# Decode attention on one core: other pieces of the K and V stream, and the last head finished on VectorE and SyncE

## The chip, the cores and the metric

The kernel runs on one core of a Trainium2 chip. The metric is the device time of one execution in microseconds (us). The core has a TensorE (PE, with its weight loads shown as PEld), a VectorE (DVE), a ScalarE (ACT), a GpSimd (POOL) and a SyncE (SP). SP and ACT each issue transfers on a queue of their own; 16 DMA engines carry them.

## The reference

```python
B, H, Sq, Sk, D = 1, 16, 1, 8192, 256      # q, k, v in bf16
scale = q.shape[-1] ** -0.5
scores = jnp.einsum("bhqd,bhkd->bhqk", q, k) * scale
p = _softmax(scores, axis=-1)
return jnp.einsum("bhqk,bhkd->bhqd", p, v)
```

There is one query per head. K and V of a head are 8192 x 256 in bf16, 4 MB each, so 16 heads read 128 MB. Every byte is used once.

## The kernel before

**Layout.** A head's 8192 keys lie as 128 partitions x 64 columns (J = 64); a column is 256 values, 512 bytes, in each partition. There are two buffers for K and two for V, chosen by the parity of the head, each 4 MB.

**The stream.** SP issues all loads in the order of the list `stream`. An entry is (k or v, head, first column, end column, semaphore). From head 2 on, the first piece of a load waits until its buffer is free: for K until VectorE is done with head h - 2 (`kd`), for V until TensorE has finished the output of head h - 2 (`pv`). SP stands at such a wait, with all later loads behind it. k0 comes in three pieces (`K_FIRST`), v0, v1 and v13 in halves, v14 in four pieces and v15 in nine (`V_LATE`), each later piece with a semaphore of its own (`V_SEMS`). From head 2 on the list goes k(h+2), v(h).

**Scores.** VectorE multiplies 48 columns of K with q and sums each (L191, one instruction per column). The last 16 columns go over TensorE: it transposes them (`ktrans`, L280), ScalarE copies them out of PSUM (L376), TensorE multiplies with q (`kscore`, L294), and ScalarE adds these scores to VectorE's (`scopy`, L380). VectorE's last column waits for that.

**Softmax.** VectorE takes the maximum per partition (`m`, L207), TensorE transposes it (`transpose_m`, L228), VectorE takes the maximum of that (`xmax`, L173), TensorE spreads it (`bcast`, L234), ScalarE takes the exponential and its sum (`expo`, L384 and L388), TensorE adds the sums (`total`, L244), and VectorE takes the reciprocal (`recips`, L178). In VectorE's program an even head runs the maximum of the head before at its column 40; an odd head has the reciprocal and the maximum of the head before at columns 2 and 3.

**Output.** `pv` (L259) multiplies 64 columns of V with the exponentials, one matmul per column, into a PSUM row of 256. `final` on ScalarE multiplies that with the reciprocal into `o_sb` (L401) and issues the store of 512 bytes (L408). TensorE works in a loop of nine turns: scores of an even head, output of the even head before, scores of the odd head, output of the odd head before. In the even output the softmax steps of the odd head before lie after columns 32, 48 and 64.

**Waits for pieces of V.** The loop's code is the same in each turn, and so are the waits in it. Before, a wait for a later piece compares a semaphore, which starts at 16, with a register: 16 in the early turns, 32 in the turn that needs the piece:

```python
fin_turn = pe.snap((i // 8) * 16 + 16)
half_turn = pe.snap(((i + 1) // 8) * 16 + 16)
```

**The end.** After its loop ScalarE finishes heads 14 and 15 with `final`, waits for both stores and stops.

Of the kernel before, what the change touches and what calls it, by code (L numbers as in the profile page):

```python
# [10 lines left out]

NPE = 16
GRP = 4
K_FIRST = (16, 32)
V_HALVED = 13
V_LATE = {14: (0, 16, 32, 48), 15: (0, 16, 28, 38, 46, 52, 57, 60, 62)}
AHEAD = {"kd": 1, "sc": 1, "sp": 2, "ex": 2, "m": 1, "g": 1, "mT": 1, "l": 2, "bc": 1, "nb": 1, "rc": 2, "pv": 2, "fin": 4}
V_SEMS = (("va0", "v0b", "v0c", "v0d"), ("va1", "v1b", "v1c", "v1d", "v1e", "v1f", "v1g", "v1i", "v1j"))


class _Step:
# [19 lines left out]
def bass_standalone__mha_softmax__decode_kernel(nc: bass.Bass, q: bass.AP, k: bass.AP, v: bass.AP, out: bass.AP):  # L41
# [3 lines left out]
    J = Sk // P  # L45
# [3 lines left out]
    NG = NPE // GRP  # L49
    JD = J - NPE  # L50
    QW = D + NH
    HALF = J // 2
    dt = k.dtype

    stream = [("k", 0, 0, K_FIRST[0], "k0"), ("k", 0, K_FIRST[0], K_FIRST[1], "k0a")]
    stream += [("k", 0, K_FIRST[1], J, "k0b"), ("k", 1, 0, J, "k1")]
    stream += [("v", 0, 0, HALF, "va0"), ("k", 2, 0, J, "k0"), ("v", 0, HALF, J, "v0c")]
    stream += [("v", 1, 0, HALF, "va1"), ("k", 3, 0, J, "k1"), ("v", 1, HALF, J, "v1c")]  # L60
    for h in range(2, H):
        if h + 2 < H:
            stream.append(("k", h + 2, 0, J, f"k{h % 2}"))
        if h in V_LATE:
            for (a, b), name in zip(zip(V_LATE[h], V_LATE[h][1:] + (J,)), V_SEMS[h % 2]):
                stream.append(("v", h, a, b, name))
        elif h == V_HALVED:
            stream += [("v", h, 0, HALF, "va1"), ("v", h, HALF, J, "v1h")]
        else:
            stream.append(("v", h, 0, J, f"va{h % 2}"))  # L70

    with contextlib.ExitStack() as ctx:
# [28 lines left out]
        identb = sb("identb", [P, P], BF16)  # L101
        ones_row = sb("ones_row", [1, P], FP32)
        ones_col = sb("ones_col", [P, 1], FP32)
        o_sb = [sb(f"o_sb{i}", [1, D], out.dtype) for i in range(2)]

        acc = [ps(f"acc{i}", [P, 512]) for i in range(2)]
# [3 lines left out]
        sm = ps("sm", [P, 512])  # L110
        qps = ps("qps", [P, 512])

        for name in ("qc", "pool", "cb", "cf", "qp", "qs", "qb", "kd", "tp", "kt", "sp", "sc", "m", "mT", "g", "bc", "nb", "ex"):
            sem(name)
        for name in ("l", "rc", "pv", "fin", "ldq", "k0", "k0a", "k0b", "k1", "va0", "va1", "v1h", "o0", "o1"):
            sem(name)
        late = [name for row in V_SEMS for name in row[1:] if name not in ("v0c", "v1c")] + ["v1h"]
        for row in V_SEMS:
            for name in row[1:]:
                sem(name)  # L120

        def src(t, h):
            return t[0, h].rearrange("(p j) d -> p (j d)", p=P)

        if True:

            @(lambda f: f(nc.sync))
            def _(sp):
                for kind, h, a, b, name in stream:
                    buf = (kbuf if kind == "k" else vbuf)[h % 2]  # L130
                    if h >= 2 and a == 0:
                        if kind == "k":
                            sp.wait_ge(sem("kd"), h)
                        else:
                            sp.wait_ge(sem("pv"), h + 1)
                    sp.dma_start(  # L136
                        buf[:, a * D : b * D], src(k if kind == "k" else v, h)[:, a * D : b * D]
                    ).then_inc(sem(name), 16)
                sp.nop()

            @(lambda f: f(nc.gpsimd))
            def _(pool):
                def step(ins, n):
                    ins.then_inc(sem("pool"), 1)
                    pool.wait_ge(sem("pool"), n)

                def eye(t, n, done):
                    step(pool.memset(t[:, :], 0.0), n)
                    pool.affine_select(
                        out=t[:, :],  # L150
                        in_=t[:, :],
                        compare_op=ALU.not_equal,
                        fill=1.0,
                        base=0,
                        pattern=[[-1, P]],
                        channel_multiplier=1,
                    ).then_inc(sem(done), 1)

                eye(identb, 1, "cb")
                eye(ident, 2, "cf")  # L160
                pool.memset(ones_row[:, :], 1.0).then_inc(sem("cf"), 1)
                pool.memset(ones_col[:, :], 1.0).then_inc(sem("cf"), 1)
                pool.memset(q_all[:, H * QW : (H + 1) * QW], 0.0).then_inc(sem("cf"), 1)
                for name, n in AHEAD.items():
                    pool.nop().then_inc(sem(name), n)
                for name in late + ["o0", "o1", "va0", "va1"]:
                    pool.nop().then_inc(sem(name), 32 if name in ("o0", "o1") else 16)

            @(lambda f: f(nc.vector))
            def _(dve):  # L170
# [9 lines left out]
                def head(h, at):  # L180
                    dve.wait_ge(sem("qb"), h.of(1, 1))
                    dve.wait_ge(sem("ex"), h.of(1, 1))
                    dve.wait_ge(sem(f"k{h.par}"), h.of(8, 16 - 8 * h.par))  # L183
                    buf = kbuf[h.par]
                    for j in range(JD):
                        if j in K_FIRST and h.par == 0:
                            dve.wait_ge(sem("k0a" if j == K_FIRST[0] else "k0b"), 16)
                        if j == JD - 1:

                            dve.wait_ge(sem("sc"), h.of(1, 2))  # L190
                        ins = dve.tensor_tensor_reduce(  # L191
                            out=buf[:, j * D : (j + 1) * D],
                            in0=buf[:, j * D : (j + 1) * D],
                            in1=q_now[h.par][:, 0:D],
                            scale=SCALE,
                            scalar=0.0,
                            op0=ALU.mult,
                            op1=ALU.add,
                            accum_out=S[h.par][:, j : j + 1],
                        )  # L200
                        if j in at:
                            at[j]()
                    ins.then_inc(sem("kd"), 1)
                    if JD in at:
                        at[JD]()
                    dve.wait_ge(sem("kd"), h.of(1, 2))
                    dve.tensor_reduce(m[:, h.par : h.par + 1], S[h.par][:, :], AX.X, ALU.max).then_inc(sem("m"), 1)  # L207
# [12 lines left out]
                recips(last.back(1))  # L220
                xmax(last)
                recips(last)

            @(lambda f: f(nc.tensor))
            def _(pe):
# [23 lines left out]
                        stop=True,  # L249
                    ).then_inc(sem("l"), 1)  # L250

                def pv(h, waits, at):

                    pe.wait_ge(sem("fin"), h.of(1, 3))
                    pe.wait_ge(sem(f"va{h.par}"), h.of(8, 32 - 8 * h.par))
                    for j in range(J):
                        for name, value in waits.get(j, ()):
                            pe.wait_ge(sem(name), value)
                        ins = pe.matmul(  # L259
                            acc[h.par][0:1, 0:D],  # L260
                            lhsT=E[h.par][:, j : j + 1],
                            rhs=vbuf[h.par][:, j * D : (j + 1) * D],
                            start=(j == 0),
                            stop=(j == J - 1),
                        )
                        if j == J - 1:
                            ins.then_inc(sem("pv"), 1)
                        if j + 1 in at:
                            at[j + 1]()
# [75 lines left out]
                pe.wait_ge(sem("cf"), 4)  # L345
                with pe.Fori(0, H // 2 + 1) as i:
                    ev, od = _Step(0, i), _Step(1, i)
                    fin_turn = pe.snap((i // 8) * 16 + 16)
                    half_turn = pe.snap(((i + 1) // 8) * 16 + 16)
                    old = od.back(2)  # L350
                    with pe.If(i < H // 2):
                        scores(ev)
                    with pe.If(i > 0):
                        pv(
                            ev.back(2),
                            {V_LATE[14][n]: [(V_SEMS[0][n], fin_turn)] for n in range(1, len(V_SEMS[0]))},
                            {32: lambda: transpose_m(old), 48: lambda: bcast(old), 64: lambda: total(old)},
                        )
                    with pe.If(i < H // 2):
                        scores(od, before=ev)  # L360
                    with pe.If(i > 0):
                        waits = {V_LATE[15][n]: [(V_SEMS[1][n], fin_turn)] for n in range(1, len(V_SEMS[1]))}
                        waits[HALF] = [("v1h", half_turn)]
                        pv(old, waits, {})
                    with pe.If(i < H // 2):
                        total(ev)

# [1 line left out]
            def _(act):  # L369
# [83 lines left out]
                                    )  # L453
                                    final(t.back(3 - d), flat[:, bass.ds(at, D)])
                expo(_Step(H - 1))
                for h in (H - 2, H - 1):
                    final(_Step(h), out[0, h, 0:1, :])
                for i in range(2):
                    act.wait_ge(sem(f"o{i}"), 16 * (H // 2 + 2))
                act.nop()  # L460


# [26 lines left out]
```

## Time and profile before

| | us |
|---|---|
| median of 3 runs | 320.18 (320.08 to 320.52) |
| the profiled execution | 320.12 |
| its span, first to last instruction | 318.6 |
| VectorE busy | 275.2 |
| TensorE matmuls busy | 219.2 |
| ScalarE busy | 92.5 |
| bytes moved | 134.29 MB, mean 422 GB/s |

The span begins with the first instruction in the profile and ends with the last. The profiled execution is 1.5 us longer than its span. A row of the timeline gives start, duration, engine, line, operation, out<-in, count, and in brackets the idle time before it and what ended it. A row of groups gives the busy time, the mean of one in ns, and the idle time before.

### The profile page before, as it was taken

How to read it: one execution, taken by the hardware profiler on the slowest of the kernel's cores; microseconds unless marked ns; L12 is line 12 of the kernel's file. 1: busy time of each engine (PE TensorE's matmuls, PEld its weight loads, DVE VectorE, ACT ScalarE, POOL GpSimd, SP SyncE). 2: the span in 40 equal slices, each digit the busy share in tenths (PEclk: the TensorE clock that was granted, in tenths of full speed). 3: DMA queues.
4: the chain of work that ended last, by engine and by line, in shares of the span. 5: the costliest groups of instructions: out<-in, count | busy, mean ns of one | idle time of the engine just before them, and what ended most of it. 6: DMA issues, size and time to landing. Idle time of an engine off the chain costs nothing.

```text
span 318.6 us, 6833 instructions
## 1 busy us (share of the span) xinstructions
PE 219.2 (69%) x2163; PEld 156.0 (49%) x2163; DVE 275.2 (86%) x1584; ACT 92.5 (29%) x172; POOL 1.6 (0%) x11
## 2 busy tenths in 40 slices
PE   4446185988775947949387482975739668497987
PEld 1335163656553634727256262663626446266664
DVE  3989999999999898897988979799798897979920
ACT  5436050333215050330505114051330603306010
POOL 1000000000000000000000000000000000000000
PEclk9999999659797875957879597695977859699999
DMA  7999999999999999999999999999999999999995
GB/s 303 447 418 465 393 455 407 448 416 448 412 448 428 428 444 411 453 412 453 420 436 440 416 448 407 453 416 449 424 432 444 411 449 416 444 405 428 419 416 201
DMA packets 6981, 134.29 MB, mean 422 GB/s; under 512 B 800, under 2 KB 1216, under 8 KB 1856
## 3 DMA queue, kind: packets, MB, share of 16 engines
q1 hardware_dynamic: 6912, 134.22, 98.6%
q8 instruction: 2, 0.03, 0.0%
q10 hardware_dynamic: 64, 0.02, 0.0%
q14 instruction: 3, 0.02, 0.0%
HBM read 134.23 MB, written 0.01 MB: 421 GB/s over the span
## 4 chain that ended last, share of the span: by engine, by line
DMA 64%; PE 19%; DVE 15%; SPq 1%; issue 1%; ACT 0%; DVEq 0%; ACTq 0%
DMA vbuf<-in_v_dram 58%; PE acc L259 18%; DVE kbuf L191 14%; DMA kbuf<-in_k_dram 7%; SPq L136 1%; DVE S L191 0%; DVE g L173 0%; PE sm L234 0%; ACT o_sb L401 0%; DVE recip L178 0%; DVEq L209 0%; DVEq L183 0%; PE qps L244 0%; DVE m L207 0%; ACTq L400 0%
## 5 line engine op out<-in xcount | busy, mean ns | idle before, releaser
L191 DVE CUSTOM_DVE_ANT_0 kbuf<-kbuf,q_now 128x256 bf16<-128x256 bf16 x768 | 268.4, 409 | 21.3 <-DMA kbuf<-in_k_dram 20.4
L259 PE MATMUL acc<-vbuf,E 128*1 128x256 bf16 x1024 | 147.1, 313 | 41.6 <-DMA vbuf<-in_v_dram 41.4
L259 PEld LDWEIGHTS acc<-vbuf,E 128*1 128x1 bf16 x1024 | 95.5, 95 | 86.2 <-DMA vbuf<-in_v_dram 44.4
L376 ACT ACTIVATE KT<-tp 128x1024 bf16<-128x1024 bf16 x64 | 62.3, 1021 | 46.4 <-PE tp L280 45.9
L191 DVE DVE_READ_ACCUMULATOR2_ANT S<- 128x1 f32 x768 | 55.2, 72 | 0.0
L280 PE MATMUL tp<-identb,kbuf 128*128 128x128 bf16 x512 | 42.2, 239 | 14.7 <-DMA kbuf<-in_k_dram 14.5
L280 PEld LDWEIGHTS tp<-identb,kbuf 128*128 128x128 bf16 x512 | 33.6, 107 | 18.1 <-DMA kbuf<-in_k_dram 12.1
L294 PE MATMUL spe<-q_now,KT 128*128 128x1 bf16 x512 | 22.9, 166 | 27.3 <-ACT KT L376 27.0
L294 PEld LDWEIGHTS spe<-q_now,KT 128*128 128x128 bf16 x512 | 18.1, 99 | 35.7 <-ACT KT L376 26.1
L401 ACT ACTIVATE o_sb<-acc,recip 1x256 bf16<-1x256 f32 x16 | 7.3, 458 | 87.0 <-PE acc L259 85.7
L384 ACT ACTIVATE negb<-sm 128x1 f32<-128x1 f32 x16 | 2.8, 174 | 83.8 <-PE sm L234 83.8
L173 DVE TENSOR_REDUCE g<-mx 1x1 f32<-1x128 f32 x16 | 4.4, 276 | 7.5 <-PE mx L228 7.5
L234 PE MATMUL sm<-g,ones_row 1*128 1x1 f32 x32 | 6.5, 268 | 5.0 <-DVE g L173 5.0
L228 PE MATMUL mx<-ident,m 128*1 128x128 f32 x32 | 6.5, 287 | 4.3 <-DVE m L207 4.3
L234 PEld LDWEIGHTS sm<-g,ones_row 1*128 1x128 f32 x32 | 5.1, 198 | 7.1 <-DVE g L173 5.6
L371 ACT ACTIVATE q_now<-q_all 128x258 bf16 x16 | 6.7, 418 | 0.1
L178 DVE RECIPROCAL recip<-qps 1x1 f32<-1x1 f32 x16 | 2.4, 152 | 3.9 <-PE qps L244 3.9
L388 ACT ACTIVATE E<-S,negb 128x64 bf16<-128x64 f32 x16 | 5.6, 348 | 0.5
L336 PE MATMUL acc<-q_sb,identb 16*128 16x256 bf16 x16 | 4.3, 404 | 0.8 <-ACT q_all L426 0.8
L228 PEld LDWEIGHTS mx<-ident,m 128*1 128x1 f32 x32 | 2.1, 82 | 5.1 <-DVE m L207 4.8
L426 ACT ACTIVATE q_all<-acc 128x512 bf16<-128x512 f32 x8 | 4.3, 592 | 0.6 <-PE acc L336 0.6
L380 ACT ACTIVATE S<-spe 128x16 f32<-128x16 f32 x16 | 2.9, 184 | 3.6 <-PE spe L294 3.6
(24 smaller groups left out, 18.5 us busy)
## 6 DMA issues: line engine op xcount, KB each, us to landing
kbuf<-in_k_dram SPq DMA_DIRECT2D x15, 4096.0 KB, 20.3
vbuf<-in_v_dram SPq DMA_DIRECT2D x11, 4096.0 KB, 28.7
vbuf<-in_v_dram SPq DMA_DIRECT2D x6, 2048.0 KB, 24.4
vbuf<-in_v_dram SPq DMA_DIRECT2D x5, 1024.0 KB, 14.8
kbuf<-in_k_dram SPq DMA_DIRECT2D x2, 1024.0 KB, 5.8
kbuf<-in_k_dram SPq DMA_DIRECT2D x1, 2048.0 KB, 11.3
vbuf<-in_v_dram SPq DMA_DIRECT2D x1, 768.0 KB, 10.2
vbuf<-in_v_dram SPq DMA_DIRECT2D x1, 640.0 KB, 11.3
```

The lines of the kernel that those rows point to most:

```text
L173: dve.tensor_reduce(g[0:1, h.par : h.par + 1], mx[0:1, 0:P], AX.X, ALU.max).then_inc(sem("g"), 1)
L191: ins = dve.tensor_tensor_reduce(out=buf[:, j * D : (j + 1) * D], in0=buf[:, j * D : (j + 1) * D], in1=q_now[h.par][:, 0:D], scale=SCALE, ...
L228: pe.matmul(mx[0:1, 0:P], lhsT=m[:, h.par : h.par + 1], rhs=ident[:, :], start=True, stop=True).then_inc(sem("mT"), 1)
L234: pe.matmul(sm[:, 0:1], lhsT=ones_row[0:1, 0:P], rhs=g[0:1, h.par : h.par + 1], start=True, stop=True,).then_inc(sem("bc"), 1)
L259: ins = pe.matmul(acc[h.par][0:1, 0:D], lhsT=E[h.par][:, j : j + 1], rhs=vbuf[h.par][:, j * D : (j + 1) * D], start=(j == 0), stop=(j == J ...
L280: ins = pe.transpose(tp[gi % 2][:, b * D + hf * P : b * D + (hf + 1) * P], buf[:, j * D + hf * P : j * D + (hf + 1) * P], identb[:, :],)
L294: ins = pe.matmul(spe[:, c : c + 1], lhsT=KT[gi % 2][:, b * D + hf * P : b * D + (hf + 1) * P], rhs=q_now[h.par][:, D + hf : D + hf + 1], ...
L336: ins = pe.matmul(acc[pair % 2][:, (h % 2) * D : (h % 2 + 1) * D], lhsT=identb[0:H, h : h + 1].to_broadcast([H, P]), rhs=q_sb[:, :], start ...
L371: act.activation(out=q_now[h.par][:, :], in_=src_q, func=ACT.Copy).then_inc(sem("qb"), 1)
L376: act.activation(out=KT[gi % 2][:, :], in_=tp[gi % 2][:, :], func=ACT.Copy).then_inc(sem("kt"), 1)
L388: act.activation(out=E[h.par][:, :], in_=S[h.par][:, :], func=ACT.Exp, bias=negb[:, h.par : h.par + 1], scale=1.0, accum_out=lsum[:, h.par ...
L401: act.activation(out=o_sb[h.par][0:1, :], in_=acc[h.par][0:1, 0:D], func=ACT.Copy, scale=recip[0:1, h.par : h.par + 1],).then_inc(sem("fin ...
```

## The change

The stream is cut in other pieces. k0 comes as columns 0 to 16 and 16 to 64. v0 and v1 are whole, and the first loads go k0, k1, v0, k2, v1, k3. v13 is cut at 34, v14 at 24 and 44, v15 at 20, 34, 44, 52, 58 and 62. The waits of `pv` for later pieces compare with the constant 16; GpSimd gives each of these semaphores a count in advance for the heads that have no such piece, and the matmul behind each wait takes 16 away. The last head's output is multiplied by the reciprocal on VectorE into a tile of its own, `o_last`, and SP issues its store, behind all loads, and waits for it.

```diff
-K_FIRST = (16, 32)
-V_HALVED = 13
-V_LATE = {14: (0, 16, 32, 48), 15: (0, 16, 28, 38, 46, 52, 57, 60, 62)}
+K_FIRST = 16
+V_LATE = {13: (0, 34), 14: (0, 24, 44), 15: (0, 20, 34, 44, 52, 58, 62)}
+V_SEMS = {13: ("va1", "v1c"), 14: ("va0", "v0b", "v0c"), 15: ("va1", "v1b", "v1c", "v1d", "v1e", "v1f", "v1g")}
-V_SEMS = (("va0", "v0b", "v0c", "v0d"), ("va1", "v1b", "v1c", "v1d", "v1e", "v1f", "v1g", "v1i", "v1j"))
...
-    stream = [("k", 0, 0, K_FIRST[0], "k0"), ("k", 0, K_FIRST[0], K_FIRST[1], "k0a")]
-    stream += [("k", 0, K_FIRST[1], J, "k0b"), ("k", 1, 0, J, "k1")]
-    stream += [("v", 0, 0, HALF, "va0"), ("k", 2, 0, J, "k0"), ("v", 0, HALF, J, "v0c")]
-    stream += [("v", 1, 0, HALF, "va1"), ("k", 3, 0, J, "k1"), ("v", 1, HALF, J, "v1c")]
+    stream = [("k", 0, 0, K_FIRST, "k0"), ("k", 0, K_FIRST, J, "k0b"), ("k", 1, 0, J, "k1")]
+    stream += [("v", 0, 0, J, "va0"), ("k", 2, 0, J, "k0"), ("v", 1, 0, J, "va1"), ("k", 3, 0, J, "k1")]
...
-        elif h == V_HALVED:
-            stream += [("v", h, 0, HALF, "va1"), ("v", h, HALF, J, "v1h")]
...
+        o_last = sb("o_last", [1, D], out.dtype)
...
+        late = {}
+        for h, names in V_SEMS.items():
+            for name in names[1:]:
                 sem(name)
+                late[name] = late.get(name, 16 * H // 2) - 16
...
+                sp.wait_ge(sem("end"), 1)
+                sp.dma_start(out[0, H - 1, 0:1, :], o_last[0:1, :]).then_inc(sem("end"), 16)
+                sp.wait_ge(sem("end"), 17)
                 sp.nop()
...
-                for name in late + ["o0", "o1", "va0", "va1"]:
-                    pool.nop().then_inc(sem(name), 32 if name in ("o0", "o1") else 16)
+                for name, n in list(late.items()) + [("o0", 32), ("o1", 32), ("va0", 16), ("va1", 16)]:
+                    pool.nop().then_inc(sem(name), n)
...
-                        if j in K_FIRST and h.par == 0:
-                            dve.wait_ge(sem("k0a" if j == K_FIRST[0] else "k0b"), 16)
+                        if j == K_FIRST and h.par == 0:
+                            dve.wait_ge(sem("k0b"), 16)
...
                 recips(last)
+                dve.wait_ge(sem("rc"), H + AHEAD["rc"])
+                dve.wait_ge(sem("pv"), H + AHEAD["pv"])
+                dve.tensor_scalar(
+                    out=o_last[0:1, :],
+                    in0=acc[last.par][0:1, 0:D],
+                    scalar1=recip[0:1, last.par : last.par + 1],
+                    scalar2=None,
+                    op0=ALU.mult,
+                ).then_inc(sem("end"), 1)
...
-                def pv(h, waits, at):
+                def pv(h, at):
 
+                    parts = dict(zip(V_LATE[H - 2 + h.par][1:], V_SEMS[H - 2 + h.par][1:]))
...
-                        for name, value in waits.get(j, ()):
-                            pe.wait_ge(sem(name), value)
+                        if j in parts:
+                            pe.wait_ge(sem(parts[j]), 16)
...
+                        if j in parts:
+                            ins.then_inc(sem(parts[j]), -16)
...
-                for h in (H - 2, H - 1):
-                    final(_Step(h), out[0, h, 0:1, :])
-                for i in range(2):
-                    act.wait_ge(sem(f"o{i}"), 16 * (H // 2 + 2))
+                final(_Step(H - 2), out[0, H - 2, 0:1, :])
+                act.wait_ge(sem("o0"), 16 * (H // 2 + 2))
+                act.wait_ge(sem("o1"), 16 * (H // 2 + 1))
```

More of the change, by code (lines that the diff above doesn't have):

```diff
@@ L51, in bass_standalone__mha_softmax__decode_kernel @@
     QW = D + NH
-    HALF = J // 2
     dt = k.dtype
-    stream = [("k", 0, 0, K_FIRST[0], "k0"), ("k", 0, K_FIRST[0], K_FIRST[1], "k0a")]
-    stream += [("k", 0, K_FIRST[1], J, "k0b"), ("k", 1, 0, J, "k1")]
-    stream += [("v", 0, 0, HALF, "va0"), ("k", 2, 0, J, "k0"), ("v", 0, HALF, J, "v0c")]
-    stream += [("v", 1, 0, HALF, "va1"), ("k", 3, 0, J, "k1"), ("v", 1, HALF, J, "v1c")]
+    stream = [("k", 0, 0, K_FIRST, "k0"), ("k", 0, K_FIRST, J, "k0b"), ("k", 1, 0, J, "k1")]
+    stream += [("v", 0, 0, J, "va0"), ("k", 2, 0, J, "k0"), ("v", 1, 0, J, "va1"), ("k", 3, 0, J, "k1")]
     for h in range(2, H):
@@ L64, in bass_standalone__mha_softmax__decode_kernel @@
         if h in V_LATE:
-            for (a, b), name in zip(zip(V_LATE[h], V_LATE[h][1:] + (J,)), V_SEMS[h % 2]):
+            for (a, b), name in zip(zip(V_LATE[h], V_LATE[h][1:] + (J,)), V_SEMS[h]):
                 stream.append(("v", h, a, b, name))
-        elif h == V_HALVED:
-            stream += [("v", h, 0, HALF, "va1"), ("v", h, HALF, J, "v1h")]
         else:
@@ L111, in bass_standalone__mha_softmax__decode_kernel @@
         qps = ps("qps", [P, 512])
-        for name in ("qc", "pool", "cb", "cf", "qp", "qs", "qb", "kd", "tp", "kt", "sp", "sc", "m", "mT", "g", "bc", "nb", "ex"):
+        for name in ("qc", "pool", "cb", "cf", "qp", "qs", "qb", "kd", "end", "tp", "kt", "sp", "sc", "m", "mT", "g", "bc", "nb", "ex"):
             sem(name)
-        for name in ("l", "rc", "pv", "fin", "ldq", "k0", "k0a", "k0b", "k1", "va0", "va1", "v1h", "o0", "o1"):
+        for name in ("l", "rc", "pv", "fin", "ldq", "k0", "k0b", "k1", "va0", "va1", "o0", "o1"):
             sem(name)
-        late = [name for row in V_SEMS for name in row[1:] if name not in ("v0c", "v1c")] + ["v1h"]
-        for row in V_SEMS:
-            for name in row[1:]:
+        late = {}
+        for h, names in V_SEMS.items():
+            for name in names[1:]:
                 sem(name)
+                late[name] = late.get(name, 16 * H // 2) - 16
         def src(t, h):
@@ L347, in _ @@
                     ev, od = _Step(0, i), _Step(1, i)
-                    fin_turn = pe.snap((i // 8) * 16 + 16)
-                    half_turn = pe.snap(((i + 1) // 8) * 16 + 16)
                     old = od.back(2)
@@ L355, in _ @@
                             ev.back(2),
-                            {V_LATE[14][n]: [(V_SEMS[0][n], fin_turn)] for n in range(1, len(V_SEMS[0]))},
                             {32: lambda: transpose_m(old), 48: lambda: bcast(old), 64: lambda: total(old)},
@@ L361, in _ @@
                     with pe.If(i > 0):
-                        waits = {V_LATE[15][n]: [(V_SEMS[1][n], fin_turn)] for n in range(1, len(V_SEMS[1]))}
-                        waits[HALF] = [("v1h", half_turn)]
-                        pv(old, waits, {})
+                        pv(old, {})
                     with pe.If(i < H // 2):
```

## The prediction

> **What bounds the kernel now.** I read the page first: which engine is full, which chain ended last.
>
> ```profile
> span 318.6 us, 6833 instructions
> ...
> PE 219.2 (69%) x2163; PEld 156.0 (49%) x2163; DVE 275.2 (86%) x1584; ACT 92.5 (29%) x172; POOL 1.6 (0%) x11
> ...
> PEclk9999999659797875957879597695977859699999
> DMA  7999999999999999999999999999999999999995
> ...
> q8 instruction: 2, 0.03, 0.0%
> q14 instruction: 3, 0.02, 0.0%
> ...
> DMA vbuf<-in_v_dram 58%; PE acc L259 18%; DVE kbuf L191 14%; DMA kbuf<-in_k_dram 7%; SPq L136 1%; DVE S L191 0%; DVE g L173 0%; PE sm L234 0%; ACT o_sb L401 0%; DVE recip L178 0%; DVEq L209 0%; DVEq L183 0%; PE qps L244 0%; DVE m L207 0%; ACTq L400 0%
> ...
> L191 DVE CUSTOM_DVE_ANT_0 kbuf<-kbuf,q_now 128x256 bf16<-128x256 bf16 x768 | 268.4, 409 | 21.3 <-DMA kbuf<-in_k_dram 20.4
> ```
>
> The transfers are busy in every slice but the first and the last; VectorE (DVE) comes second. So the time is a start, one unbroken stream of 128 MB, and a tail, and a change counts only if it alters the number of pieces in the stream, opens a hole in it, or alters the tail. The timeline gives the pace of the stream wherever a consumer waited for a landing:
>
> ```profile
> 13.03 1.86 PE L280 MATMUL tp<-identb,kbuf 128*128 128x128 bf16 x16 [3.96 <-DMA kbuf<-in_k_dram]
> 23.25 1.63 PEld L280 LDWEIGHTS tp<-identb,kbuf 128*128 128x128 bf16 x16 [0.62 <-DMA kbuf<-in_k_dram]
> 38.79 1.89 PE L280 MATMUL tp<-identb,kbuf 128*128 128x128 bf16 x16 [8.53 <-DMA kbuf<-in_k_dram]
> ...
> 121.47 6.05 PE L259 MATMUL acc<-vbuf,E 128*1 128x256 bf16 x32 [4.62 <-DMA vbuf<-in_v_dram]
> 140.90 10.06 PE L259 MATMUL acc<-vbuf,E 128*1 128x256 bf16 x64 [3.71 <-DMA vbuf<-in_v_dram]
> ...
> 286.63 1.07 PE L280 MATMUL tp<-identb,kbuf 128*128 128x128 bf16 x16 [0.20 <-DMA kbuf<-in_k_dram]
> 296.42 3.65 PE L259 MATMUL acc<-vbuf,E 128*1 128x256 bf16 x32 [0.77 <-DMA vbuf<-in_v_dram]
> 308.85 8.04 PE L259 MATMUL acc<-vbuf,E 128*1 128x256 bf16 x64 [0.55 <-DMA vbuf<-in_v_dram]
> ```
>
> Between 121.47 and 140.90 land two whole heads (k7, v5): 9.715 us per 4 MB. The two halves of v13 take 296.42-286.63 = 9.79, 0.08 more for one extra piece. From 296.42 to 308.85 five 1 MB pieces land (v14 and the first of v15): 2.486 each, 9.94 for a head in four pieces, 0.23 more for three extra pieces. So a further piece costs 0.077 us of stream.
>
> The tail, with PE's weight loads showing the landing of each piece of v15:
>
> ```profile
> 310.74 1.18 PEld L259 LDWEIGHTS acc<-vbuf,E 128*1 128x1 bf16 x12 [0.28 <-DMA vbuf<-in_v_dram]
> 312.32 0.96 PEld L259 LDWEIGHTS acc<-vbuf,E 128*1 128x1 bf16 x10 [0.41 <-DMA vbuf<-in_v_dram]
> 313.62 0.74 PEld L259 LDWEIGHTS acc<-vbuf,E 128*1 128x1 bf16 x8 [0.34 <-DMA vbuf<-in_v_dram]
> 314.63 0.52 PEld L259 LDWEIGHTS acc<-vbuf,E 128*1 128x1 bf16 x6 [0.27 <-DMA vbuf<-in_v_dram]
> 315.41 1.18 PEld L259 LDWEIGHTS acc<-vbuf,E 128*1 128x1 bf16 x12 [0.26 <-DMA vbuf<-in_v_dram]
> 316.97 0.47 ACT L401 ACTIVATE o_sb<-acc,recip 1x256 bf16<-1x256 f32 x1 [8.15 <-PE acc L259]
> 317.47 0.24 ACTq L408 DMA_DIRECT2D out_dram<-o_sb  x1
> ```
>
> PE keeps pace until 315.41; then the last 12 columns run without a wait. Estimate: the last 7 columns of the stream take 7/64 x 9.715 = 1.06 us after 315.41, so the stream ends at about 316.45. PE is done some 0.45 later (ScalarE starts at 316.97), and 1.63 us go from there to the span's end. The last landing to the end is about 2.1 us. The transfers of this window, in 40 slices of 0.215 us, show one thing more:
>
> ```profile
> DMA  9999999999999999999953322120000000000000
> ```
>
> From 314.5 on only 0.2 to 0.3 of the 16 engines work: four engines end about 1.5 us after the others, and the last decides.
>
> **The change, part by part.**
>
> *Pieces.* The stream goes from 48 transfers to 42: k0, v0, v1 and v14 lose one each, v15 two; v13 keeps two. Four at 0.077 are -0.31 us. In v15, the five pieces from 308.85 to 315.41 carry 41 columns in 6.56 us against 41/64 x 9.715 = 6.22, 0.07 per piece; but two of the small last pieces go, where the estimate above needed no extra at all. So between 0 and -0.14 for two; I take -0.07. Together -0.38.
>
> *Start.* VectorE has 16 columns of k0 as before, at 0.35 us each (268.4/768):
>
> ```profile
> 5.54 0.42 DVE L191 CUSTOM_DVE_ANT_0 kbuf<-kbuf,q_now 128x256 bf16<-128x256 bf16 x1 [5.54 <-DMA kbuf<-in_k_dram]
> 22.26 0.33 SPq L136 DMA_DIRECT2D kbuf<-in_k_dram  x1
> 40.27 0.33 SPq L136 DMA_DIRECT2D kbuf<-in_k_dram  x1
> 57.96 0.33 SPq L136 DMA_DIRECT2D kbuf<-in_k_dram  x1
> 59.69 0.33 SPq L136 DMA_DIRECT2D vbuf<-in_v_dram  x1
> 75.69 0.33 SPq L136 DMA_DIRECT2D kbuf<-in_k_dram  x1
> ```
>
> They end at 11.1. The rest of k0 is now one piece and is there at 12.95 (PE sees it at 13.03 now), so VectorE stands 1.85 us and k2 is issued at 24.1, not 22.26. This is hidden: v0, now whole and ahead of k2, keeps the queue full until about 33.6 (23.25 + 10.35, with the lateness that k2 shows at 38.79). k3 is issued 16.9 after head 1 starts, at about 41.4; v1 fills the queue until 53.
>
> *Order.* The first places are now k1, v0, k2, v1, k3, k4. k2 lands about 43.5 (38.79 + half a head), k3 at 62.9. Head 2 starts at 43.6, and 17.0 to 17.1 us after the landing of its k its buffer is free: the issue of k4 comes at 60.6. Here, without v1's second half between k3 and k4, the queue holds 2.3 us of work. What must be covered is issue to flow: 0.74 to 5.54 was 4.8 us for k0's first 1 MB at 2.49, so 2.3 us, cold and with the last engine counted. So k4 just arrives; k5, 19.4 us later, stands the same (k3 at 62.9, issue at 80.0, v2 ends at 82.3). I take +0.1 for the two, between 0 and +0.6 (0.3 each). PE causes no more delay there: its first output product ends about 62.3 (59.69 + 2.6), before head 3 needs its sum at 63.7. From k6 on, margins grow by two us per head.
>
> *PE's waits.* Constants in place of register values, and a decrement that rides on a matmul. Hidden: PE waits for V in nearly every head (3.7 and 4.6 us in the rows above). In the tail that cover is gone. There today's register waits let PE start within 0.05 us of a landing (the gaps of 0.26 to 0.41 are the rest of PE's wait), and the 16 transposes at 13.03, with a signal after the eighth, run on as one row without a gap. So I take 0, between -0.05 and +0.1.
>
> *The tail's pieces.* 20, 14, 10, 8, 6, 4, 2 columns land, from the last one back, at 0, -0.37, -1.05, -2.03, -3.31, -4.90, -7.09 us (0.152 per column and 0.07 per piece). PE needs 0.11 per column (the weight loads: 1.18 for 12, 0.74 for 8, 0.52 for 6) and 0.04 to react: it runs from -7.05 to -4.85, and the next pieces' columns end at -3.3, -2.2, -1.1, -0.35 and +0.1; the last two end at +0.3, and the product is complete 0.2 later (today: 12 columns from 315.41 give 316.73, ScalarE starts at 316.97), so at +0.5. Without the 0.07 for the last small pieces the earlier ones land closer to the end, and it is +0.6; it was 0.45. I take +0.10.
>
> *VectorE for ScalarE, SP for ACT.*
>
> ```profile
> L401 ACT ACTIVATE o_sb<-acc,recip 1x256 bf16<-1x256 f32 x16 | 7.3, 458 | 87.0 <-PE acc L259 85.7
> L173 DVE TENSOR_REDUCE g<-mx 1x1 f32<-1x128 f32 x16 | 4.4, 276 | 7.5 <-PE mx L228 7.5
> L178 DVE RECIPROCAL recip<-qps 1x1 f32<-1x1 f32 x16 | 2.4, 152 | 3.9 <-PE qps L244 3.9
> 303.72 0.22 DVE L207 TENSOR_REDUCE m<-S 128x1 f32<-128x64 f32 x1
> ```
>
> VectorE reading PSUM costs 152 ns for one element and 276 for 128: 0.98 ns each, so 400 ns for 256, between 276 and 458. Against the 0.47 at 316.97 that is -0.07. [...] VectorE has had nothing to do since its last reduction at 303.72 but two small reciprocals, and SP's last load went out before 304; nothing queues behind either. SP's issue takes 0.33 against ACTq's 0.24; if the store waits for that, +0.09, else 0: I take +0.05.
>
> *Sum.* -0.38 + 0.10 + 0.10 - 0.07 + 0.05 = -0.20. The profiled execution took 320.12 (span 318.6 and 1.5 around it), so 319.92; it lies 0.06 under the median of 320.18, which gives 319.98. I say 319.95.
>
> **Rivals.**
>
> *The queue runs dry at k4 and k5 (slower).* The margin at both is near 0. If issue to flow is longer than 2.3 us, or head 2 is held up (its maximum waits for PE's 32 columns of head 0, which the later k2 brings to within a us), each us is lost on all engines, and k5 repeats it. With 0.6 lost at each, +1.2 in place of +0.1: 321.0. It decides from 0.45 us at each. For it: two places with no slack, where 5 us of v1 lay before k4 (issue 57.96). Against: the 2.3 are the cold figure, and only the four late engines count.
>
> *Instruction loads (slower or faster).* Five instruction loads (q8, q14) fall in the run; an engine that serves one ends its share late, and that is my reading of the four late engines. If the changed code puts two on one engine, it ends later still by about 0.9: 320.9; if the latest is spared, the next one decides, up to 0.7 less: 319.3. For the code being laid out alike: few instructions change. [...]
>
> *PE's clock halves in the tail (slower).* The clock row dips to 5 to 7 tenths where PE waits 3.7 to 4.6 us for V; a column costs up to twice 0.11 there. Half of v15 at that pace leaves PE 2 us or more behind: 322. Against: the row shows 9 in the last five slices, and the gaps that I reckon in the tail stay under 1.2 us.
>
> *Pieces cost more than the rows say (faster).* If the tail's merged pieces and the early ones each give 0.15, the stream is 0.9 shorter: 319.4.
>
> **How the numbers follow.** About 0.2%, 0.64 us, is what a measurement can tell here. My forecast, 319.5 to 320.8 with the bounds of the unknown terms, has 0.62. Dry queue beyond 0.64: 0.14; a doubled instruction load: 0.06; the clock: 0.04; together 0.24 slower. Faster by instruction loads 0.07, by pieces 0.07: 0.14. The range 319.45 to 321.05 leaves out the clock, the worst of the dry queue and the best of the faster cases.
>
> **What would show it.** Right: the first wait on VectorE for k0 near 11; k4 issued near 60.6 and k5 near 80, with no hole in the transfers near 62 or 82; the second half of v13 seen by PE about 0.25 us earlier than 296.42; a 0.40 us tensor-scalar on VectorE at about 316.7, then SP's store. Wrong: a hole at 62, landings after 100 us that are later than before, or a tail in which PE waits for other pieces than these.

## The result: slower by 0.3%, and scattered

| | median us | lowest to highest |
|---|---|---|
| before | 320.11 | 320.02 to 320.52 |
| changed | 321.17 | 320.08 to 322.18 |

The ratio is 1.0030, 95% interval 1.0022 to 1.0039. Each kernel ran 22 times. The changed kernel is not slower by a fixed amount: a third of its executions lie within 0.5 us of the one before, the others up to 2 us above. The profiled execution, at 321.51, is one of the longer ones; its span is 320.2 us.

The page of the changed kernel, in the parts that were quoted before:

```profile
span 320.2 us, 6866 instructions
...
DMA  8999999999999999999999999999999999999994
GB/s 325 453 400 454 409 438 438 364 418 434 422 426 446 414 450 434 418 446 413 450 430 422 446 409 450 426 430 446 405 454 422 434 442 409 454 403 424 425 395 196
...
q8 instruction: 2, 0.03, 0.0%
...
q14 instruction: 3, 0.02, 0.0%
```

The kernel before moved this much in the same slices:

```profile
GB/s 303 447 418 465 393 455 407 448 416 448 412 448 428 428 444 411 453 412 453 420 436 440 416 448 407 453 416 449 424 432 444 411 449 416 444 405 428 419 416 201
```

In 40 slices of 8 us the busy share of the transfers still looks full, and there are five instruction loads as before. The GB/s hint at a place: 364 in the eighth slice (56 to 64 us), where no slice of the kernel before but the first and the last is under 393. The loss must be looked for where it begins, and the timeline of PE has a good place: PE waits for the landing of v4 in both kernels. First the changed kernel, then the one before, then two experiments that come below (the changed kernel with v0 alone in halves, and with v1 alone in halves):

```profile
122.95 6.54 PE L267 MATMUL acc<-vbuf,E 128*1 128x256 bf16 x32 [3.04 <-DMA vbuf<-in_v_dram]
```

```profile
121.47 6.05 PE L259 MATMUL acc<-vbuf,E 128*1 128x256 bf16 x32 [4.62 <-DMA vbuf<-in_v_dram]
```

```profile
124.00 5.40 PE L271 MATMUL acc<-vbuf,E 128*1 128x256 bf16 x32 [3.61 <-DMA vbuf<-in_v_dram]
```

```profile
121.34 6.45 PE L271 MATMUL acc<-vbuf,E 128*1 128x256 bf16 x32 [4.09 <-DMA vbuf<-in_v_dram]
```

The changed kernel is 1.48 us behind at v4, and about as much at its end: 1.39 us by the times (321.51 against 320.12), 1.6 by the spans (320.2 against 318.6). So the loss was there before 123 us, and the nearly 200 us after it, with the new pieces of v13 to v15 and the new end, neither lost nor gained much. SP's own rows in the changed kernel say which transfers lie there:

```profile
24.15 0.33 SPq L132 DMA_DIRECT2D kbuf<-in_k_dram  x1
24.52 0.43 SPq L132 DMA_DIRECT2D vbuf<-in_v_dram  x1
41.21 19.68 SPq L132 DMA_DIRECT2D kbuf<-in_k_dram  x2
62.28 0.33 SPq L132 DMA_DIRECT2D vbuf<-in_v_dram  x1
80.12 0.33 SPq L132 DMA_DIRECT2D kbuf<-in_k_dram  x1
80.50 0.43 SPq L132 DMA_DIRECT2D vbuf<-in_v_dram  x1
```

The third row holds two issues, k3 at 41.21 and k4, whose issue ends at 60.89. k5 goes out at 80.12. The busy times by stage have the transfers' share and GB/s in their last two columns. The changed kernel, the one before, and the changed kernel with the queue kept full between k3 and k4 (an experiment below):

```profile
56.00:66.00 10.00, 6.90 (x52) 4.79 (x53) 7.60 (x45) 2.50 (x5) 0.00 (x0) 0.66 0.90 364
80.00:84.00 4.00, 1.99 (x40) 1.56 (x40) 3.49 (x21) 3.88 (x4) 0.00 (x0) 1.00 0.95 385
```

```profile
56.00:66.00 10.00, 8.57 (x89) 6.14 (x90) 9.54 (x56) 5.05 (x12) 0.00 (x0) 0.67 1.05 451
80.00:84.00 4.00, 2.19 (x25) 1.37 (x24) 4.00 (x23) 1.83 (x4) 0.00 (x0) 0.75 1.01 434
```

```profile
56.00:66.00 10.00, 6.26 (x60) 4.71 (x58) 7.59 (x45) 2.55 (x5) 0.00 (x0) 0.87 1.00 428
80.00:84.00 4.00, 1.99 (x40) 1.57 (x40) 3.49 (x21) 3.88 (x4) 0.00 (x0) 1.00 1.07 459
```

364 GB/s from 56 to 66 us and 385 from 80 to 84, where the others move 428 to 459: less behind the issue of k4, and less behind that of k5. VectorE and PE do the same in these stages with more work in the queue (3.49 and 1.99 us busy from 80 to 84), so a slower VectorE or PE is not the reason. These sums show that little was queued, not what it costs. An experiment below without the loss (v0 and v1 in halves again) moves 410 and 402 GB/s in the two stages, and an execution of 320.02 with the whole first loads moves 354 and 393.

The cost shows in the landings. The trace has sixteen of them for each load, as many as there are DMA engines, and they are read here as one part per engine. The sixteen parts of k4 land from 72.2 to 72.7 us in the changed kernel, and from 70.9 to 72.8 before: the early engines waited at k4, the last one lost nothing. Of k5, fifteen parts land from 91.8 to 92.4 (before: 90.4 to 92.1), the sixteenth at 93.8 (before: 92.3). The packets say the same: fifteen engines begin k5 between 81.6 and 82.05, one at 83.08, and the loads behind k5 keep this one late part (of v4, fifteen land by 121.5 and one at 122.9). So the loss of this execution is 1.5 us on one engine, at its start of k5.

### The profile page after: what moved, and what is told of

It is laid out like the page before. It is cut to its first block, busy times and chain, and to the rows that moved or that the text cites. A ratio compares the mean times of both kernels' runs of the same rounds, so it can differ in the third digit from the quotient of the medians.

```text
span 320.2 us, 6866 instructions
## 1 busy us (share of the span) xinstructions
PE 220.3 (69%) x2163; PEld 157.4 (49%) x2163; DVE 275.6 (86%) x1585; ACT 92.0 (29%) x171; POOL 1.6 (0%) x11
## 4 chain that ended last, share of the span: by engine, by line
DMA 54%; PE 25%; DVE 18%; issue 1%; ACT 1%; SPq 0%; DVEq 0%; ACTq 0%
DMA vbuf<-in_v_dram 43%; PE acc L267 23%; DVE kbuf L189 17%; DMA kbuf<-in_k_dram 10%; PE sm L241 1%; DVE S L189 1%; ACT KT L381 1%; PE mx L235 0%; PE tp L290 0%; PE spe L304 0%; DVE g L172 0%; DVE o_last L223 0%; SPq L132 0%; DVE recip L177 0%; DVEq L207 0%
```

## The experiments

Theory: at k4 and k5 the queue runs dry or nearly so, and a DMA engine that starts again may be late by a varying time; the stream's end is that of its latest engine. Rival A: instruction loads that fall on one DMA engine. Rival B: the late pieces of V, or PE's clock near the tail.

**The first loads undone.** The changed kernel with v0 and v1 in halves again:

```diff
-    stream += [("v", 0, 0, J, "va0"), ("k", 2, 0, J, "k0"), ("v", 1, 0, J, "va1"), ("k", 3, 0, J, "k1")]
+    stream += [("v", 0, 0, HALF, "va0"), ("k", 2, 0, J, "k0"), ("v", 0, HALF, J, "v0h")]
+    stream += [("v", 1, 0, HALF, "va1"), ("k", 3, 0, J, "k1"), ("v", 1, HALF, J, "v1h")]
...
+                        if j == HALF and h.par in (0, 1):
+                            pe.wait_ge(sem(f"v{h.par}h"), 16)
```

> The changed kernel, with v0 and v1 in halves around k2 and k3 as before (one constant wait more per head in TensorE's loop). Theory (the queue runs dry at k4 and k5, and a restart leaves some engine late by a varying amount): no hole near 61 and 81 us, 320.0 (319.8 to 320.3), runs close together. Rival A (instruction loads doubled on one engine): about 321.1 as the changed kernel, scattered. Rival B (pieces of v13 to v15, or the clock of TensorE near the tail): about 321.1.

Measured: 320.08 (319.93 to 321.06), ratio 1.0003 (0.9994 to 1.0012). The loss of the median is gone with all the rest of the change in place. The runs are not as close together as expected: four of eleven lie above 320.3, one of them at 321.06, and no trace here says why.

**The first loads alone.** The kernel before, with only this edit:

```diff
-    stream += [("v", 0, 0, HALF, "va0"), ("k", 2, 0, J, "k0"), ("v", 0, HALF, J, "v0c")]
-    stream += [("v", 1, 0, HALF, "va1"), ("k", 3, 0, J, "k1"), ("v", 1, HALF, J, "v1c")]
+    stream += [("v", 0, 0, J, "va0"), ("k", 2, 0, J, "k0"), ("v", 1, 0, J, "va1"), ("k", 3, 0, J, "k1")]
```

> The kernel before, with v0 and v1 whole in the order k0, k1, v0, k2, v1, k3, k4, and nothing else of the change. Theory: slower by 0.6 to 1.2 us (320.7 to 321.3), runs scattered over 1 to 2 us, holes near 61 and 81. Rivals A and B: 320.0, two pieces fewer, no scatter.

Measured: median 320.42, 320.16 to 322.66 over 12 executions, ratio 1.0028 (1.0012 to 1.0044). The median is below what was expected; the scatter is like the changed kernel's (four executions lie above 321.8), and the interval of the ratio contains the changed kernel's 1.0030. The profiled execution is a short one, 320.33: its two stages move 367 and 393 GB/s, as in the changed kernel, but k5's last part lands at 92.6, only 0.3 us later than before. Both directions name the order of the first loads; rivals A and B, which would have left the loss in the first and none here, fall.

**One hole at a time.** The changed kernel with v0 alone in halves (k2 early, k4 covered, k5 not), then with v1 alone in halves (k5 covered, k4 not).

```diff
-    stream += [("v", 0, 0, J, "va0"), ("k", 2, 0, J, "k0"), ("v", 1, 0, J, "va1"), ("k", 3, 0, J, "k1")]
+    stream += [("v", 0, 0, HALF, "va0"), ("k", 2, 0, J, "k0"), ("v", 0, HALF, J, "v0h")]
+    stream += [("v", 1, 0, J, "va1"), ("k", 3, 0, J, "k1")]
```

> The changed kernel with v0 alone in halves: k2 is there 5 us earlier, so k4 is issued with 5 us of work in the queue and only k5 meets an almost empty queue. Theory: a hole near 81 alone; 320.2 to 320.9, between the two. Rivals A and B: 321.1.

```diff
-    stream += [("v", 0, 0, J, "va0"), ("k", 2, 0, J, "k0"), ("v", 1, 0, J, "va1"), ("k", 3, 0, J, "k1")]
+    stream += [("v", 0, 0, J, "va0"), ("k", 2, 0, J, "k0")]
+    stream += [("v", 1, 0, HALF, "va1"), ("k", 3, 0, J, "k1"), ("v", 1, HALF, J, "v1h")]
```

> The changed kernel with v1 alone in halves: k4 meets a queue with about 2 us of work, k5 one with about 5. Theory: a hole near 61 alone. If the restart at k5 does the damage, since at k4 the late engines are still behind and cover it: 320.0 to 320.3; if any restart does it: 320.5 to 321.2. Rivals A and B: 321.1.

Measured: v0 halved 322.00 (321.62 to 322.45), ratio 1.0055 (1.0042 to 1.0068), worse than the change itself; v1 halved 320.33 (319.93 to 321.73), ratio 1.001 (1.0001 to 1.002). The stages again, with v0 halved and then with v1 halved:

```profile
56.00:66.00 10.00, 7.20 (x48) 5.02 (x48) 5.80 (x35) 2.45 (x5) 0.00 (x0) 0.50 0.99 406
80.00:84.00 4.00, 2.18 (x47) 1.75 (x48) 3.49 (x21) 3.69 (x4) 0.00 (x0) 0.90 0.80 287
```

```profile
56.00:66.00 10.00, 7.85 (x99) 5.97 (x96) 9.96 (x59) 4.47 (x8) 0.00 (x0) 0.98 0.97 395
80.00:84.00 4.00, 1.90 (x16) 1.21 (x17) 4.00 (x25) 0.81 (x3) 0.00 (x0) 0.50 1.01 434
```

The deep hole (287 GB/s) is at k5 in the first. For k4 the landings say more than 406 and 395 GB/s do: with v0 halved k4's parts land from 70.9 to 72.9 us, as before, and with v1 halved from 72.1 to 72.7, the early engines having waited. So little work at k5 costs up to 2 us, and little work at k4 by itself 0.2 of median, which the scatter hardly tells from nothing. That the first comes out above the full change was in no theory. A reading that fits: at k4 in the changed kernel the early DMA engines wait and so draw level with the late ones, which the landings show, and at k5 the latest then has less to lose, which was not tried. Where the two kernels' rows stand at v4 (124.00 and 121.34 above) is again where they stand at the end (322.45 and 319.93).

**The hole filled in another way.** The changed kernel with 2 MB more, into a tile that nobody reads, between k3 and k4:

```diff
+                    if (kind, h) == ("k", 4):
+                        sp.dma_start(filler[:, :], src(v, 1)[:, 0 : J // 2 * D]).then_inc(sem("fill"), 16)
```

> The changed kernel with a load of 2 MB into a tile that nobody reads, between k3 and k4 in SP's order: it adds 4.9 us of stream and keeps the queue full at k4 and k5. Theory (the restarts cost the time): 324.8 to 325.1, that is 320.0 plus 4.9, little scatter, no hole near 61 or 81. If the order of v0 and v1 costs in another way: 326.0 (321.2 plus 4.9) with the scatter of the changed kernel.

Measured: 324.88 (324.77 to 324.93), ratio 1.0147 (1.0132 to 1.0163). Half of 9.715 is 4.86, so without the extra bytes it would be 320.02. The order is the changed one; only the queue is full. The loss is gone, and so is the scatter as far as four executions can tell. That shows the theory's first half: what costs the time is too little work in the queue, not the order of the loads as such.

**The other parts alone.** The kernel before with the new end, and the kernel before with the new pieces of v13 to v15 and the constant waits.

```diff
+                dve.tensor_scalar(out=o_last[0:1, :], in0=acc[last.par][0:1, 0:D], ...).then_inc(sem("end"), 1)
...
+                sp.dma_start(out[0, H - 1, 0:1, :], o_last[0:1, :]).then_inc(sem("end"), 16)
```

> The kernel before with the new end alone: VectorE multiplies the last output, SP stores it. By the profile of the changed kernel (472 ns on VectorE against 465 on ScalarE, store to end 1.15 us against 1.1): +0.05 to +0.15 us, 320.2. By the prediction's step (400 ns): -0.02, 320.1. If the end were the cause of the loss: 320.9 or more.

```diff
+V_LATE = {13: (0, 34), 14: (0, 24, 44), 15: (0, 20, 34, 44, 52, 58, 62)}
...
+                            pe.wait_ge(sem(parts[j]), 16)
...
+                            ins.then_inc(sem(parts[j]), -16)
```

> The kernel before with the pieces of v13, v14 and v15 and the constant waits of the changed kernel alone; first loads and end as before. By the prediction's steps (stream 0.15 shorter, TensorE 0.15 later at its end): 320.1. If TensorE's clock is half near v13, so that v15 is issued late, and this were the cause of the loss: 320.5 to 321.5.

Measured: new end 320.04 (319.97 to 320.24), ratio 0.9998 (0.9989 to 1.0007); late pieces 320.13 (320.06 to 320.26), ratio 1.0000 (0.9991 to 1.0009). Neither differs from the kernel before beyond its interval. The rows of the new end in the first of them:

```profile
317.08 0.47 DVE L229 TENSOR_SCALAR o_last<-acc,recip 1x256 bf16<-1x256 f32 x1 [8.52 <-PE acc L272]
317.58 0.32 SPq L141 DMA_DIRECT2D out_dram<-o_last  x1
```

VectorE needs what ScalarE needed (0.47), and from SP's issue to the span's end at 318.7 it is 1.1 us, as from ACT's (317.47 to 318.6).

**Why a restart is late: two tries.** SP issues v3 0.4 us behind k5. The first try put 60 empty instructions between them, in the kernel with v0 in halves.

```diff
+                    if (kind, h) == ("v", 3):
+                        for _ in range(60):
+                            sp.nop()
```

> The changed kernel with v0 alone in halves (322.0) and a pause of some us on SP between the issues of k5 and v3, made of empty instructions. If a restart of an engine at k5 is late since SP hands out v3's load right behind k5's, the pause takes that away: 320.2 to 320.8. If the late restart does not depend on the next issue: 321.6 to 322.4 as without the pause.

Measured: 321.23 (320.86 to 321.50), ratio 1.0032 (1.0021 to 1.0043). It tells nothing of the next issue, since the trace shows no pause: k5 at 80.15, v3 at 80.52. What it does show is that the loss moves by 0.8 us between two kernels that issue alike: this one is no slower than the changed kernel, while v0 in halves without the empty instructions was. The second try makes SP wait for a step that comes later, once in the kernel with v0 in halves, once in the changed kernel:

```diff
                             sp.wait_ge(sem("pv"), h + 1)
+                            if h == 3:
+                                sp.wait_ge(sem("sc"), 6)
```

> The changed kernel with v0 alone in halves, and SP issues v3 only when ScalarE has copied head 4's last scores: by the trace about 84.5 us, 4 us after k5, and 7 us before the queue needs it. If one engine restarts late at k5 since v3's load is handed out right behind k5's: 320.1 to 320.6, all engines flow by 82.5. If the late restart has nothing to do with the next issue: 321.1 to 322.4, as the two runs without a real pause.

> The changed kernel with the same later issue of v3. If the late restart comes of the next issue: 319.9 to 320.5, little scatter. If not: 320.2 to 322 as the changed kernel, median about 321.1.

```profile
80.15 0.33 SPq L136 DMA_DIRECT2D kbuf<-in_k_dram  x1
84.88 0.33 SPq L136 DMA_DIRECT2D vbuf<-in_v_dram  x1
```

Measured: 322.07 (321.37 to 322.73), ratio 1.0065 (1.0052 to 1.0078), and 321.20 (320.02 to 322.34), ratio 1.0037 (1.0019 to 1.0055). With v3 4.7 to 5.1 us behind k5 nothing is better: the next issue is not the cause. The changed kernel with the late v3 was profiled in one of its low executions (320.02), and shows that the same program can get away with it:

```profile
121.44 5.90 PE L269 MATMUL acc<-vbuf,E 128*1 128x256 bf16 x32 [3.80 <-DMA vbuf<-in_v_dram]
```

The landings of k5 put the runs side by side, in us, each for its profiled execution:

| kernel | k5 issued | fifteen parts land | last part lands | time |
|---|---|---|---|---|
| before | 75.69 | 90.4 to 92.1 | 92.3 | 320.12 |
| changed | 80.12 | 91.8 to 92.4 | 93.8 | 321.51 |
| changed, v0 and v1 in halves | 76.38 | 90.4 to 92.2 | 92.3 | 319.95 |
| before, v0 and v1 whole | 80.11 | 91.7 to 92.3 | 92.6 | 320.33 |
| changed, v0 in halves | 80.18 | 91.9 to 93.1 | 94.8 | 322.45 |
| changed, v1 in halves | 77.62 | 91.5 to 92.1 | 92.2 | 319.93 |
| changed, hole filled | 80.22 | 95.1 to 97.0 | 97.1 | 324.87 |
| v0 in halves, empty instructions | 80.15 | 91.8 to 93.2 | 93.6 | 321.39 |
| v0 in halves, v3 later | 80.15 | 91.8 to 92.7 | 93.6 | 321.37 |
| changed, v3 later | 80.08 | 91.8 to 92.2 | 92.3 | 320.02 |

From the landing of k5's last part to the end it is 227.6 to 227.8 us in each of them. So what sets these executions apart is settled when k5 has landed, and with k5 issued near 80.1 and nothing added to the queue one late engine decides it, in some executions and not in others.

**A candidate.** The kernel before with the new end and with k0 in two pieces (`K_FIRST = 16`), the parts that did not lose:

> The kernel before with the new end and with k0 in two pieces, VectorE waiting near 11 us for the second. By the measured parts (new end 320.04) and one piece of 0.08 us less: 319.95 to 320.1, scatter as before; a candidate to beat both kernels. If the wait at k0 delays k4 and opens a hole there: 320.3 to 321.

Measured: 320.00 (319.83 to 320.48), ratio 1.0000 (0.9991 to 1.0008). The median is 0.1 us lower, the scatter is larger than with the new end alone; no gain is shown. No version here beats the kernel before beyond its interval.

## Why the prediction was wrong

The forecast was 319.95, no change; the measured median, 321.17, lies 0.1 above the range. The step that failed is the one called *Order*: its term for the issues of k4 and k5, +0.1 us and at most +0.6, where the runs show about 1.1 (321.17 against 320.08 with the first loads undone).

**What held.** The stream bounds the kernel, and the times of the issues came as worked out: VectorE waits for k0's second piece until 12.97 (12.95 forecast),

```profile
12.97 0.42 DVE L189 CUSTOM_DVE_ANT_0 kbuf<-kbuf,q_now 128x256 bf16<-128x256 bf16 x1 [1.70 <-DMA kbuf<-in_k_dram]
```

k2 at 24.15 (24.1), k3 at 41.2 (41.4), k4 at 60.6 (60.6), k5 at 80.12 (80.0). The place without slack was named, and so was the rival that came true, at a chance of 0.14, and one of the signs of being wrong: landings after 100 us that come later. That the rival's price, 321.0, is so near the 321.17 measured is luck. It counted 0.6 us on all engines at each of two places; in the profiled execution the last engine lost nothing at k4, and one engine lost 1.5 us at k5.

**What failed.** The 2.3 us from issue to flow were taken as the cold, and so the worst, case; no row gave the bound of 0.3 at each place. In the profiled execution v4 lands 1.48 late although three pieces fewer lie ahead of it (0.23 by the prediction's own price), so the latest engine lost 1.7: from the issue of k5 at 80.12 it flowed not at 82.3 but near 84.0, 3.9 us behind the issue. The landing of k5's last part at 93.8, less 9.7 for the load, gives the same 84. By the same reckoning it was about 5 us with v0 halved (124.00). One read of a start says how long a start can take, not how long it can take at most; and where the slack is the same as that one number, a chance of 0.14 for a dry queue was too low. Nor is the price the same on all engines, as the rival had it, nor confined to the four late engines, as the argument against it had it. The engines had drawn level at k4, and fifteen of them took up k5 within 2 us of its issue; the one that did not set the end.

**The other terms.** The fewer pieces (-0.38) are not seen as a gain in any run: those of v0 and v1 can't be told from the loss at k5, k0's one came to 320.00 against 320.04, within the scatter, and the late pieces came to 0 with TensorE's longer end, where -0.05 was the sum. The new end was put at -0.02 (-0.07 for VectorE, +0.05 for SP); it measures -0.1 with 0 well inside the interval. VectorE's 400 ns, read off a line through 152 and 276 ns, were 472:

```profile
L223 DVE TENSOR_SCALAR o_last<-acc,recip 1x256 bf16<-1x256 f32 x1 | 0.5, 472 | 7.0 <-PE acc L267 7.0
```

That is no gain over ScalarE's 465.

**The other rivals.** The instruction loads are five in both kernels, and none of the changed kernel's falls between 56 and 88 us, where the loss arises: they start between 18.17 and 37.28. In the kernel before they start between 14.51 and 36.09; there the last piece of k0 lands in sixteen parts from 12.5 to 12.9, and of k2 twelve parts land from 36.8 to 37.2 and four from 37.9 to 38.7, which fits the prediction's reading of the four late engines. The 0.9 and 0.7 us that it put on a doubled or a spared load were its author's estimates; no run shows them. PE's clock did fall, though not in the tail but before it: from 293.7 to 303.7 us the granted clock is 0.71 in the changed kernel and 1.00 before, and PE makes v13's 64 columns in 10 us,

```profile
293.67 10.01 PE L267 MATMUL acc<-vbuf,E 128*1 128x256 bf16 x64
...
303.71 4.04 SPq L132 DMA_DIRECT2D vbuf<-in_v_dram  x7
...
311.22 7.20 PE L267 MATMUL acc<-vbuf,E 128*1 128x256 bf16 x64
```

so that v15 is issued at 303.71, not 300.10. That is a third place with about 2 us of work in the queue: fifteen parts of v14's last piece land from 305.8 to 306.3. Of v15's first piece twelve parts land from 308.9 to 309.5, four from 310.1 to 310.8. The engine that was late since k5 hides it (the sixteenth part of v14's last piece lands at 307.7), and it cost nothing that shows; the last 64 columns run at 0.11 each. Why the clock is lower there was not tried.

## What to carry to other kernels

A stream that is always busy in a profile can stand on a few places with little queued work; count for each issue how many us of transfers lie ahead of it, and take the least. Here 2.3 us to the last landing ahead (v2 at 82.4, k5 issued at 80.12) were too little in most executions, and 4.4 us (v1 at 63.1, k4 issued at 58.66 with the first loads undone) were enough for a median of 320.08. No run lies between the two. The one start read from the trace, 2.3 us, was not the longest: by the reckoning above one engine flowed 3.9 us behind the issue of k5, the other fifteen began within 2 us of it, and the one set the end. So set the work that lies ahead against the slowest start that the landings show, not against one read of a start. A split load that looks like waste (0.08 us a piece here) may be what holds about 5 us of work in the queue.

## What the runs showed that was not expected

Too little work in the queue made this kernel scatter: with it executions lie 2 us apart, with the 2 MB more 0.16 us (four executions) and with the first loads undone 1.1 us. It need not hurt all engines: in the changed kernel fifteen of sixteen went on with k5 almost without a pause (v2's parts land from 81.9 to 82.4, k5 begins between 81.6 and 82.05) and one fell behind (83.08). By the last landing less 9.7 us, the flow of k5 began from 2.5 us (92.3, issued at 80.08) to 4.9 us (94.8, issued at 80.18) behind the issue, and it is not the next issue that delays it (322.07 and 321.20 with v3 4.7 to 5.1 us behind k5). What delays it stays open. So does whether little work at k5 costs more without the wait at k4: 322.00 and 322.07 say so, 321.23 does not.
